# One transposing DMA in place of several, one more segment of x turned on TensorE, and an output bank lent to side work

## The chip, the cores and the metric

The kernel runs on one core of a Trainium2 chip. The metric is the device time of one execution in microseconds (us). TensorE (PE) multiplies, ScalarE (ACT) does the exponentials, VectorE (DVE) copies, normalises and reduces, GpSimd (POOL) masks, and SyncE (SP) issues every DMA. Each engine runs its own instructions strictly in order.

## What is computed

Two blocks on inputs of 2048 x 1024 bf16, their results side by side. A is plain attention with 32 heads of width 32. B is attention over four segments of 512 rows, causal within a segment, with a compressive memory carried from segment to segment and a gate per head.

```python
# A
qkv = (x @ wqkv) -> q, k, v per head
o_A = softmax(q @ k.T * Dh**-0.5) @ v;   out_A = o_A @ wo
# B, for s in range(4):
a_dot = softmax(q_s @ k_s.T * Dh**-0.5 + mask) @ v_s
a_mem = (phi(q_s) @ M) / (phi(q_s) @ z + 1e-6)
o     = g * a_mem + (1 - g) * a_dot        # g = sigmoid(beta)
M    += phi(k_s).T @ v_s;   z += sum(phi(k_s))   # phi(t) = t + 1 if t > 0 else exp(t)
out_B = concat(o) @ wo
```

## The kernel before

**Tiling.** Heads go in groups of four (128 columns of the weights), eight groups g. For A, each group has K, Q and V projections over four chunks c of 512 rows (`a_prep`), and then eight units of 256 queries each. For B there are 32 steps n = 8 s + g (`b_prep`), one for each segment s and group g, each with two units. A unit's scores come out of PE transposed, keys on partitions (`emit_scores`, L453); ACT takes the exponential of two or three PSUM banks at once into a ring PT of 20 slots (L470); then `emit_pv` (L519) multiplies by V and by ones, accumulating output and denominator in PSUM bank 5 (`OLB`). Banks 0 to 4 hold scores, and banks 6 and 7 (`PROJ`) serve everything else: projections, turns on PE, norms, the memory's products, output projections.

**Turns.** Projections need x with its columns on partitions. Of A's x, twelve of the sixteen 128-row tiles are loaded as they are into OTA, which is free at the start (`stage`), and turned on PE by `turn` (L373: eight transposes into one bank, then one copy out, on DVE and ACT alternately). B's first segment is turned likewise; its four tiles use places 12 to 15 of OTA. The last four tiles of A's x (chunk 3), and the later segments of B's x (`load_xB`, L318), come by eight transposing DMAs each of 512 x 128. V is projected transposed (columns on partitions), copied to VT (A) or SQB[1] (B), and turned by `turn_V` (L609) with four transposing DMAs of 128 x 128, each into its own tile of VA or VB; phi(K) is turned in the same way into PKt, for the memory's update (L811), in the first three segments.

**What sets the order.** The program is written out in Python before it runs. `schedule` keeps a model of when every engine will be free and when every operation ends. PE's modelled time is its clock: in each round it emits scores if a pair or triple of banks is free and the ring has room, else side work (generators such as `a_prep`, sorted by priority) or the next P V product, which are taken strictly in order from `pvq`. An operation is emitted only when the model has its operands ready. On the chip the recorded order is fixed, and semaphores hold an instruction (and all behind it on its engine) until its operands are really there. For a DMA, `Recorder.dma` books SP for `issue` us, then a shared pipe for `mb`/0.2 us, and 1.5 us more to landing; `turn_V` gives 0.6 us an issue and 0.06 MB, `load_xB` 1.3 us and 0.125 MB. Each of 24 DMA semaphores is used in turn, and a DMA waits for the last one on its own semaphore.

**Start.** `loads` issues on SP, in order: two of B's weights, B's four tiles, A's K weight, A's tiles 0 to 3, two more weights, A's tiles 4 to 11, eight transposing DMAs for chunk 3, the last weight, and four tiny DMAs that spread beta over partitions. Loads for the next step, the turns of V, phi(K) and the later segments of x, and the stores follow on the same queue, in the order in which the planner emits them. A first PV product needs its V tile, so the accumulation bank stands unused until V of B's first step is there.

Of the kernel before, what the change touches and what calls it, by code (L numbers as in the profile page):

```python
# [35 lines left out]
class Recorder:  # L36
# [58 lines left out]
    def dma(self, fn, r=(), w=(), issue=0.1, mb=0.25):  # L95
        c = self.ch_next
        self.ch_next = (c + 1) % self.NCH
        op = Op(f"D{c}", self.ch_n[c], fn)
        self.ch_n[c] += 1
        op.deps = self._deps(op.eng, r, w)  # L100
        if self.ch_last[c] is not None:
            op.deps.append(self.ch_last[c])
        self.ch_last[c] = op
        op.dma = c
        self._note(op, r, w)
        t = self.free["SP"]
        for d in op.deps:
            t = max(t, d.end + LAT)
        self.free["SP"] = t + issue
        self.pipe = max(self.pipe, t + issue) + mb / 0.2  # L110
        op.end = self.pipe + 1.5
        self.all.append(op)
        return op
# [121 lines left out]
class Kernel:  # L235
# [78 lines left out]
    def load_xB(self, s):  # L314
        b = s % len(self.xB)
        for i in range(NI):
            src = self.B_x[0][512 * s:512 * s + 512, P * i:P * i + P]
            self.R.dma(lambda e, i=i, src=src: e.dma_start(self.xB[b][:, i, :], src, transpose=True),  # L318
                       w=[("xB", b, i)], issue=1.3, mb=0.125)
        self.events.add(("xB", s))  # L320

    def stage(self, k):

        keys = [("OTA", k // 2, 4 * (k % 2) + c) for c in range(4)]
        return self.OTA[:, k // 2, 1024 * (k % 2):1024 * (k % 2) + 1024], keys

    def loads(self):
        R = self.R
        nc = self.nc
        for k in range(2):  # L330
            self.load_WB(k, 0)
        for k in range(4):
            dst, keys = self.stage(12 + k)
            R.dma(lambda e, k=k, dst=dst: e.dma_start(dst, self.B_x[0][P * k:P * k + P, :]), w=keys, issue=0.5)
        self.events.add(("xB", 0))
        self.load_WA(0, 0)
        for k in range(12):
            dst, keys = self.stage(k)
            R.dma(lambda e, k=k, dst=dst: e.dma_start(dst, self.A_x[0][P * k:P * k + P, :]), w=keys, issue=0.5)
            if k == 3:  # L340
                self.load_WA(1, 0)
                self.load_WB(2, 0)
        c = 3
        for i in range(NI):
            src = self.A_x[0][512 * c:512 * c + 512, P * i:P * i + P]
            R.dma(lambda e, i=i, c=c, src=src: e.dma_start(self.xA[:, i, 512 * c:512 * c + 512], src, transpose=True),
                  w=[("xA", i, c)], issue=1.3, mb=0.125)
        self.load_WA(2, 0)
        for h in range(4):
            src = bass.AP(tensor=self.B_beta.tensor, offset=self.B_beta.offset + h, ap=[[0, 32], [4, NG]])  # L350

            def f(e, h=h, src=src):
                with nc.allow_non_contiguous_dma(reason="tiny beta broadcast"):
                    return e.dma_start(self.beta[32 * h:32 * h + 32, 0:NG], src)
            R.dma(f, w=[("beta", h)], issue=0.5, mb=0.01)

# [26 lines left out]
    def constants(self):  # L383
# [19 lines left out]
        for i in range(2):  # L403
            pool(lambda e, i=i: e.memset(self.VB[i][:, :, :], 1.0), [("VB", i, t) for t in range(4)])
        pool(lambda e: e.memset(self.maskbd[:, :], 1.0), ["maskbd"])
# [94 lines left out]
    def emit_pv(self, u, st, part):  # L500
        R = self.R
        b = u.buf
        end = st == len(u.steps) - 1 and part == 1
        t, q0, w, off = u.steps[st][part]
        mms = []
        for ones in (False, True):
            for h in range(4):
                hs = slice(32 * h, 32 * h + 32)
                rhs = self.PT[:, u.p[(st, h)], off:off + w]
                if ones:  # L510
                    lhsT, o = self.ones[:, 0:32], self.ps[hs, OLB, QC + q0:QC + q0 + w]
                else:
                    lhsT = self.VA[b][:, t, hs] if u.kind == "A" else self.VB[b][:, t, hs]
                    o = self.ps[hs, OLB, q0:q0 + w]
                mms.append((o, lhsT, rhs, st == 0 and part == 0 and not ones))

        def f(e):
            for o, l, r, start in mms:
                ins = e.matmul(o, l, r, start=start, stop=end, skip_group_check=True)  # L519
            return ins  # L520
        vk = [("VA", b, t // 4, t % 4)] if u.kind == "A" else [("VB", b, t)]
        R.op("PE", f, r=[("PT", u.p[(st, h)]) for h in range(4)] + vk + ["ones"], w=[("ps", OLB)],
             cost=0.02 + 2 * w * 0.000417, mode="C")
        if part == 1:
            for h in range(4):
                self.ring_busy.discard(u.p[(st, h)])
        if end:
            x = u.seq % 2
            R.op("DVE", lambda e: e.tensor_copy(self.OL[x][:, :], self.ps[:, OLB, :]), r=[("ps", OLB)], w=[("OL", x)], cost=0.66)  # L529
            self.spawn(self.finish(u), -1, f"fin{u.kind}{u.kn}")  # L530
# [75 lines left out]
    def turn_V(self, src, skey, dst, dkey):  # L606

        for t in range(4):
            self.R.dma(lambda e, t=t: e.dma_start(dst[:, t, :], src[:, P * t:P * t + P], transpose=True),  # L609
                       r=[skey], w=[dkey + (t,)], issue=0.6, mb=0.06)  # L610

# [31 lines left out]
    def a_prep(self, g):  # L643
# [17 lines left out]
        def proj_V(c):  # L661
            vt, key = self.VT[c % 2], ("VT", c % 2)
            cs = slice(512 * c, 512 * c + 512)
            yield from self.proj_T(self.WA[2], ("WA", 2), lambda i: self.xA[:, i, cs], lambda i: ("xA", i, c), vt[:, :], key)
            self.turn_V(vt, key, self.VA[b][:, 4 * c:4 * c + 4, :], ("VA", b, c))
            self.events.add(("vA", g, c))
# [6 lines left out]
        for c in range(4):  # L673
            yield pace()
            if g == 0 and c < 3:
                yield from self.turn([(4 * c + t, self.xA[:, :, P * (4 * c + t):P * (4 * c + t) + P], [("xA", i, c) for i in range(NI)])
# [39 lines left out]
    def b_prep(self, n):  # L716
# [8 lines left out]
        if n == 0:  # L725
            yield from self.turn([(12 + t, self.xB[0][:, :, P * t:P * t + P], [("xB", 0, i) for i in range(NI)]) for t in range(4)])
        for k in range(2):
# [22 lines left out]
        yield from self.proj_T(self.WB[2], ("WB", 2), lambda i: self.xB[xb][:, i, :], xk, self.VTB[:, :], ("SQB", 1))  # L750
        self.turn_V(self.VTB, ("SQB", 1), VB[:, :, 0:P], ("VB", b))
        self.events.add(("vB", n))
# [48 lines left out]
        if s < 3:  # L801

            self.turn_V(PH[:, 0, :], ("PH", b), self.PKt, ("PKt",))
            yield ("t", R.lastw[("PKt", 3)].end)
            op = R.lastw[("PKt", 3)]
            bank = yield ("bank",)
            yield ("pe", op.end + 0.1)

            def fm(e, bank=bank):
                for tl in range(4):  # L810
                    ins = e.matmul(self.ps[:, bank, 0:129], self.PKt[:, tl, :], VB[:, tl, 0:129], start=(tl == 0), stop=(tl == 3))  # L811
                return ins
            R.op("PE", fm, r=[("PKt", t) for t in range(4)] + [("VB", b, t) for t in range(4)], w=[("ps", bank)], cost=0.4)
            op = R.op("DVE", lambda e, bank=bank: e.tensor_tensor(self.Mf[:, g, :], self.Mf[:, g, :], self.ps[:, bank, 0:129], ALU.add),
# [39 lines left out]
    def satisfied(self, req, now):  # L854
# [4 lines left out]
        if k == "bank":  # L859
            return any(b not in self.bank_busy and self.bank_end[b] <= now + 0.1 for b in PROJ)  # L860
        if k == "out":
# [11 lines left out]
    def resume(self, task, room=0.0):  # L873
        val = room
        if task.req[0] == "bank":
            now = self.R.free["PE"]
            val = next(b for b in PROJ if b not in self.bank_busy and self.bank_end[b] <= now + 0.1)
            self.bank_busy.add(val)
# [25 lines left out]
    def schedule(self):  # L904
# [7 lines left out]
        self.slot_end = {s: 0.0 for s in SLOTS}  # L912
        self.bank_busy, self.bank_end = set(), {b: 0.0 for b in PROJ}
        self.spawn(self.gates(), (-1, 0), "gates")
# [5 lines left out]
        while True:  # L920
# [37 lines left out]
            for what in (("pv", "side") if full else ("side", "pv")):  # L958
                if done:
                    break  # L960
                if what == "pv" and self.pvq:
# [3 lines left out]
                    v = ("vA", u.g, t // 4) if u.kind == "A" else ("vB", u.kn)  # L965
                    vk = ("VA", u.buf, t // 4, t % 4) if u.kind == "A" else ("VB", u.buf, t)
                    if v in ev and self.ready([vk]) <= now and all((st, h) in u.pend for h in range(4)) \
# [3 lines left out]
                            and (c <= room or len(self.ring_busy) > RING - 4):  # L971
                        self.emit_pv(u, st, part)
                        self.pvq.pop(0)
                        done = True
                elif what == "side":
# [8 lines left out]
            if cur is None and not self.qA and not self.qB and not self.pvq and not self.tasks:  # L984
                break
            bank = next((b for b in PROJ if b not in self.bank_busy and self.bank_end[b] <= now), None)
            if now < 45 and (RING - 1) not in self.ring_busy and not self.pos_ring and gap >= 0.3 and bank is not None:
# [57 lines left out]
```

## Time and profile before

| | us |
|---|---|
| median of three runs | 1438.58 |
| lowest and highest | 1428.88 and 1440.39 |
| the profiled execution | 1436.34 |
| its span in the profile | 1434.6 |
| granted TensorE clock, mean | 0.944 |
| bytes moved by DMA | 66.46 MB |

How to read it: the span is cut in windows, and for each engine the time in which it was busy stands in them. A row of the timeline gives the start, the length of a run of equal instructions, engine, line and operation, what it writes and reads, the count, and in brackets how long the engine stood idle before and what ended that. "SPq" rows are times in which SP's queue issued a DMA; they are not the time of the transfer. Where a run of instructions goes on without a bracket, the engine had no idle time worth naming before it.

### The profile page before, as it was taken

To read this page: it belongs to the slowest core of one execution; us is meant where nothing else is said; L and a number is where in the kernel's file an instruction comes from. 1 tells how busy PE (TensorE), PEld (TensorE's weight loads), DVE (VectorE), ACT (ScalarE), POOL (GpSimd) and SP (SyncE) were. 2 spreads that over 40 slices of the span, in tenths; PEclk is the share of its full clock that TensorE was granted. 3 is DMA by queue.
4 is the path that set the end of the run, shared out by engine and by line. 5 is a ranking of instruction groups with operands and counts; after the bars stand their busy time and mean duration, and the time that the engine had idled before them with its cause. 6 is when DMAs were issued, how large, how long until landed. Compare 5 with 4: busy or idle time off the path is not lost.

```text
span 1434.6 us, 37694 instructions
## 1 busy us (share of the span) xinstructions
PE 1258.9 (88%) x16930; PEld 511.7 (36%) x17155; DVE 833.0 (58%) x1389; ACT 1208.3 (84%) x1035; POOL 114.8 (8%) x209
## 2 busy tenths in 40 slices
PE   5678998898889997889769899899889989999998
PEld 3323333333333332333323333333334333333343
DVE  3446444645567646656446565466757758466675
ACT  3258798898889997899769999799989999999930
POOL 1000000101020101110001110001100101011110
PEclk9899899899999997989978999999999999999999
DMA  7224202112311012110320111211121011321111
GB/s 191 53 43 125 48 14 55 38 24 52 65 42 39 16 35 54 33 32 16 53 52 17 34 35 28 48 42 26 31 48 34 20 33 34 101 57 35 27 56 67
DMA packets 208770, 66.46 MB, mean 46 GB/s; under 512 B 200416, under 2 KB 200416, under 8 KB 208608
## 3 DMA queue, kind: packets, MB, share of 16 engines
q1 hardware_dynamic: 208608, 64.03, 19.1%
q8 instruction: 135, 2.21, 0.6%
q14 instruction: 27, 0.22, 0.1%
HBM read 39.85 MB, written 8.39 MB: 34 GB/s over the span
## 4 chain that ended last, share of the span: by engine, by line
ACT 54%; PE 26%; SPq 8%; DVE 5%; DMA 5%; issue 2%; DVEq 0%; ACTq 0%
ACT PT L470 53%; PE ps L593 13%; SPq L609 6%; PE ps L453 6%; PE ps L519 6%; SPq L318 2%; DMA PKt<-PH 1%; DVE OL L539 1%; DMA VB<-SQB 1%; DMA VA<-VT 1%; ACT E L763 1%; DMA WB<-in_B_wk_dram 1%; DVE OL L529 1%; DVE den L789 1%; PE ps L373 1%
## 5 line engine op out<-in xcount | busy, mean ns | idle before, releaser
L470 ACT ACTIVATE PT<-ps,cbA 128x1024 bf16<-128x1024 f32 (+1 forms) x832 | 1014.4, 1359 | 104.9 <-PE ps L453 93.9
L453 PE MATMUL ps<-QA,KA 32*128 32x256 bf16 x4096 | 334.6, 280 | 27.0 <-ACT PT L470 16.5
L519 PE MATMUL ps<-PT,ones 128*32 128x256 bf16 (+1 forms) x4864 | 323.2, 279 | 0.0
L519 PE MATMUL ps<-PT,VA 128*32 128x256 bf16 x4096 | 280.1, 285 | 8.9 <-DMA VA<-VT 6.3
L539 DVE RECIPROCAL OL<-OL 128x128 f32<-128x128 f32 x256 | 242.8, 949 | 5.4
L593 PE MATMUL ps<-xB,WB 128*128 128x512 bf16 x681 | 190.9, 397 | 29.5 <-issue 12.4
L593 PE MATMUL ps<-xA,WA 128*128 128x512 bf16 x685 | 189.0, 394 | 23.7 <-issue 11.8
L453 PEld LDWEIGHTS ps<-QA,KA 32*128 32x128 bf16 x4096 | 96.3, 93 | 303.7 <-ACT PT L470 230.7
L470 ACT ACTIVATE PT<-ps,cbB 128x768 bf16<-128x768 f32 (+3 forms) x160 | 170.6, 1183 | 35.9 <-PE ps L453 28.7
L490 POOL TENSOR_SCALAR_AFFINE_SELECT PT<-PT 128x512 bf16<-128x512 bf16 (+2 forms) x145 | 85.1, 601 | 1035.9 <-ACT PT L470 1034.6
L519 PEld LDWEIGHTS ps<-PT,VA 128*32 128x32 bf16 x4096 | 109.2, 96 | 147.2 <-issue 126.6
L519 PEld LDWEIGHTS ps<-PT,ones 128*32 128x32 bf16 x4864 | 132.6, 98 | 4.0 <-issue 0.2
L529 DVE COPY OL<-ps 128x512 f32<-128x512 f32 x128 | 86.1, 673 | 75.0 <-PE ps L519 74.3
L593 PEld LDWEIGHTS ps<-xB,WB 128*128 128x128 bf16 x768 | 63.7, 100 | 103.6 <-issue 47.0
L593 PEld LDWEIGHTS ps<-xA,WA 128*128 128x128 bf16 x768 | 61.8, 99 | 96.9 <-issue 37.2
L789 DVE RECIPROCAL den<-den 128x128 f32<-128x128 f32 x96 | 91.1, 949 | 2.2
L603 DVE CAST KQB<-ps 128x512 bf16<-128x512 f32 x64 | 43.3, 676 | 74.4 <-PE ps L593 73.8
L603 DVE CAST VT<-ps 128x512 bf16<-128x512 f32 x32 | 21.7, 677 | 91.3 <-PE ps L593 55.2
L838 DVE CAST outsb<-ps 128x512 bf16<-128x512 f32 x64 | 43.5, 682 | 51.0 <-PE ps L593 45.7
L593 PE MATMUL ps<-WoB,OTB 128*128 128x512 bf16 x238 | 63.4, 398 | 5.6 <-issue 2.7
L453 PE MATMUL ps<-KQB 32*128 32x256 bf16 (+1 forms) x768 | 59.6, 267 | 5.8 <-ACT PT L470 4.4
L593 PE MATMUL ps<-xA,OTA 128*128 128x512 bf16 x242 | 58.6, 380 | 3.5 <-issue 1.7
(72 smaller groups left out, 671.4 us busy)
## 6 DMA issues: line engine op xcount, KB each, us to landing
WB<-in_B_wk_dram SPq DMA_DIRECT2D x32, 256.0 KB, 3.1
WB<-in_B_wq_dram SPq DMA_DIRECT2D x32, 256.0 KB, 3.4
WB<-in_B_wv_dram SPq DMA_DIRECT2D x32, 256.0 KB, 3.1
out_dram<-outsb SPq DMA_DIRECT2D x32, 256.0 KB, 2.1
WA<-in_A_wqkv_dram SPq DMA_DIRECT2D x24, 256.0 KB, 3.8
OTA<-in_A_x_dram SPq DMA_DIRECT2D x12, 256.0 KB, 5.7
VB<-SQB SPq DMA_TRANSPOSE x128, 2.4
VA<-VT SPq DMA_TRANSPOSE x128, 2.4
```

Of the source, the lines that this page charges most:

```text
L318: self.R.dma(lambda e, i=i, src=src: e.dma_start(self.xB[b][:, i, :], src, transpose=True), w=[("xB", b, i)], issue=1.3, mb=0.125)
L453: ins = e.matmul(o, l, r, start=True, stop=True)
L470: op = R.op("ACT", lambda e: e.activation(self.PT[:, s0:s0 + n, 0:width], self.ps[:, banks[0]:banks[0] + n, 0:width], ACTF.Exp, bias=cb, s ...
L490: mo = R.op("POOL", lambda e, ap=ap, pat=pat: e.affine_select(ap, ap, pattern=pat, compare_op=ALU.is_ge, fill=0.0, base=0, channel_multipl ...
L519: ins = e.matmul(o, l, r, start=start, stop=end, skip_group_check=True)
L529: R.op("DVE", lambda e: e.tensor_copy(self.OL[x][:, :], self.ps[:, OLB, :]), r=[("ps", OLB)], w=[("OL", x)], cost=0.66)
L539: R.op("DVE", lambda e, Lq=Lq: e.reciprocal(Lq, Lq), r=[k], w=[k], cost=0.87)
L593: ins = e.matmul(o, l, rh, start=a, stop=z)
L603: op = self.R.op("DVE", lambda e: e.tensor_copy(dst, self.ps[:, bank, :]), r=[("ps", bank)], w=[dkey], cost=0.66)
L609: self.R.dma(lambda e, t=t: e.dma_start(dst[:, t, :], src[:, P * t:P * t + P], transpose=True), r=[skey], w=[dkey + (t,)], issue=0.6, mb=0.06)
L789: R.op("DVE", lambda e, cs=cs: e.reciprocal(self.den[:, cs], self.den[:, cs]), r=["den"], w=["den"], cost=0.9)
L838: op = R.op("DVE", lambda e, ns=ns, bank=bank, ob=ob: e.tensor_copy(self.outsb[ob][:, ns], self.ps[:, bank, :]), r=[("ps", bank)], w=[("ou ...
```

## The change

One transposing DMA does the work of four in `turn_V`, and one that of eight in `load_xB`; the planner's bookings and the names under which readiness is kept follow (a V or phi(K) tile is ready when the whole of it is). Chunk 3 of A's x is loaded as it is and turned on PE like the others; for that A's sixteen tiles fill OTA's places and B's four first tiles go to OTB[0]. The order of the first loads changes: beta comes after A's tile 3, and B's second weight after B's second tile. `self.banks` replaces PROJ: it holds banks 6 and 7 and, until the first P V product is emitted, bank 5 as well. The planner's pipe is booked at 0.25 MB a us.

```diff
-        self.pipe = max(self.pipe, t + issue) + mb / 0.2
+        self.pipe = max(self.pipe, t + issue) + mb / 0.25
...
     def load_xB(self, s):
         b = s % len(self.xB)
-        for i in range(NI):
-            src = self.B_x[0][512 * s:512 * s + 512, P * i:P * i + P]
-            self.R.dma(lambda e, i=i, src=src: e.dma_start(self.xB[b][:, i, :], src, transpose=True),
-                       w=[("xB", b, i)], issue=1.3, mb=0.125)
+        src = self.B_x[0][512 * s:512 * s + 512, :]
+        self.R.dma(lambda e: e.dma_start(self.xB[b][:, :, :], src, transpose=True),
+                   w=[("xB", b, i) for i in range(NI)], issue=5.0, mb=1.0)
...
     def stage(self, k):
-        keys = [("OTA", k // 2, 4 * (k % 2) + c) for c in range(4)]
-        return self.OTA[:, k // 2, 1024 * (k % 2):1024 * (k % 2) + 1024], keys
+        if k < 16:
+            return self.OTA[:, k // 2, 1024 * (k % 2):1024 * (k % 2) + 1024], [("OTA", k // 2, 4 * (k % 2) + c) for c in range(4)]
+        k -= 16
+        flat = self.OTB[0][:, :, :].rearrange("p j n -> p (j n)")
+        return flat[:, 1024 * k:1024 * k + 1024], [("OTB", 0, 2 * k), ("OTB", 0, 2 * k + 1)]
...
     def loads(self):
-        for k in range(2):
-            self.load_WB(k, 0)
+        self.load_WB(0, 0)
         for k in range(4):
-            dst, keys = self.stage(12 + k)
-            R.dma(lambda e, k=k, dst=dst: e.dma_start(dst, self.B_x[0][P * k:P * k + P, :]), w=keys, issue=0.5)
+            tile_in(16 + k, self.B_x[0][P * k:P * k + P, :])
+            if k == 1:
+                self.load_WB(1, 0)
         self.load_WA(0, 0)
-        for k in range(12):
+        for k in range(16):
+            tile_in(k, self.A_x[0][P * k:P * k + P, :])
             if k == 3:
+                for h in range(4):
+                    R.dma(f, w=[("beta", h)], issue=0.5, mb=0.01)
+            if k == 7:
                 self.load_WA(1, 0)
                 self.load_WB(2, 0)
-        c = 3
-        for i in range(NI):
-            src = self.A_x[0][512 * c:512 * c + 512, P * i:P * i + P]
-            R.dma(lambda e, i=i, c=c, src=src: e.dma_start(self.xA[:, i, 512 * c:512 * c + 512], src, transpose=True),
-                  w=[("xA", i, c)], issue=1.3, mb=0.125)
         self.load_WA(2, 0)
-        for h in range(4):
-            R.dma(f, w=[("beta", h)], issue=0.5, mb=0.01)
...
     def turn_V(self, src, skey, dst, dkey):
-        for t in range(4):
-            self.R.dma(lambda e, t=t: e.dma_start(dst[:, t, :], src[:, P * t:P * t + P], transpose=True),
-                       r=[skey], w=[dkey + (t,)], issue=0.6, mb=0.06)
+        self.R.dma(lambda e: e.dma_start(dst, src, transpose=True), r=[skey], w=[dkey], issue=1.4, mb=0.2)
...
-            if g == 0 and c < 3:
+            if g == 0:
                 yield from self.turn(...)
...
+        self.banks = PROJ + [OLB]
...
-                        self.emit_pv(u, st, part)
-                        self.pvq.pop(0)
-                        done = True
+                        if OLB in self.banks and OLB not in self.bank_busy:
+                            self.banks.remove(OLB)
+                        if OLB not in self.banks:
+                            self.emit_pv(u, st, part)
+                            self.pvq.pop(0)
+                            done = True
```

More of the change, by code (lines that the diff above doesn't have):

```diff
@@ L329, in loads, with tile_in, f @@
         nc = self.nc
-        for k in range(2):
-            self.load_WB(k, 0)
+        def tile_in(k, src):
+            dst, keys = self.stage(k)
+            R.dma(lambda e: e.dma_start(dst, src), w=keys, issue=0.5)
+        self.load_WB(0, 0)
         for k in range(4):
-            dst, keys = self.stage(12 + k)
-            R.dma(lambda e, k=k, dst=dst: e.dma_start(dst, self.B_x[0][P * k:P * k + P, :]), w=keys, issue=0.5)
+            tile_in(16 + k, self.B_x[0][P * k:P * k + P, :])
+            if k == 1:
+                self.load_WB(1, 0)
         self.events.add(("xB", 0))
         self.load_WA(0, 0)
-        for k in range(12):
-            dst, keys = self.stage(k)
-            R.dma(lambda e, k=k, dst=dst: e.dma_start(dst, self.A_x[0][P * k:P * k + P, :]), w=keys, issue=0.5)
+        for k in range(16):
+            tile_in(k, self.A_x[0][P * k:P * k + P, :])
             if k == 3:
+                for h in range(4):
+                    src = bass.AP(tensor=self.B_beta.tensor, offset=self.B_beta.offset + h, ap=[[0, 32], [4, NG]])
+                    def f(e, h=h, src=src):
+                        with nc.allow_non_contiguous_dma(reason="tiny beta broadcast"):
+                            return e.dma_start(self.beta[32 * h:32 * h + 32, 0:NG], src)
+                    R.dma(f, w=[("beta", h)], issue=0.5, mb=0.01)
+            if k == 7:
                 self.load_WA(1, 0)
                 self.load_WB(2, 0)
-        c = 3
-        for i in range(NI):
-            src = self.A_x[0][512 * c:512 * c + 512, P * i:P * i + P]
-            R.dma(lambda e, i=i, c=c, src=src: e.dma_start(self.xA[:, i, 512 * c:512 * c + 512], src, transpose=True),
-                  w=[("xA", i, c)], issue=1.3, mb=0.125)
-        self.load_WA(2, 0)
-        for h in range(4):
[L350 to L354, printed above, removed]
-            R.dma(f, w=[("beta", h)], issue=0.5, mb=0.01)
+        self.load_WA(2, 0)
     def late_loads(self):
@@ L403, in constants @@
         for i in range(2):
-            pool(lambda e, i=i: e.memset(self.VB[i][:, :, :], 1.0), [("VB", i, t) for t in range(4)])
+            pool(lambda e, i=i: e.memset(self.VB[i][:, :, :], 1.0), [("VB", i)])
         pool(lambda e: e.memset(self.maskbd[:, :], 1.0), ["maskbd"])
@@ L520, in f @@
             return ins
-        vk = [("VA", b, t // 4, t % 4)] if u.kind == "A" else [("VB", b, t)]
+        vk = [("VA", b, t // 4)] if u.kind == "A" else [("VB", b)]
         R.op("PE", f, r=[("PT", u.p[(st, h)]) for h in range(4)] + vk + ["ones"], w=[("ps", OLB)],
@@ L664, in proj_V @@
             yield from self.proj_T(self.WA[2], ("WA", 2), lambda i: self.xA[:, i, cs], lambda i: ("xA", i, c), vt[:, :], key)
-            self.turn_V(vt, key, self.VA[b][:, 4 * c:4 * c + 4, :], ("VA", b, c))
+            self.turn_V(vt[:, :], key, self.VA[b][:, 4 * c:4 * c + 4, :], ("VA", b, c))
             self.events.add(("vA", g, c))
@@ L725, in b_prep @@
         if n == 0:
-            yield from self.turn([(12 + t, self.xB[0][:, :, P * t:P * t + P], [("xB", 0, i) for i in range(NI)]) for t in range(4)])
+            yield from self.turn([(16 + t, self.xB[0][:, :, P * t:P * t + P], [("xB", 0, i) for i in range(NI)]) for t in range(4)])
         for k in range(2):
@@ L750, in b_prep @@
         yield from self.proj_T(self.WB[2], ("WB", 2), lambda i: self.xB[xb][:, i, :], xk, self.VTB[:, :], ("SQB", 1))
-        self.turn_V(self.VTB, ("SQB", 1), VB[:, :, 0:P], ("VB", b))
+        self.turn_V(self.VTB[:, :], ("SQB", 1), VB[:, :, 0:P], ("VB", b))
         self.events.add(("vB", n))
@@ L801, in b_prep @@
         if s < 3:
-            self.turn_V(PH[:, 0, :], ("PH", b), self.PKt, ("PKt",))
-            yield ("t", R.lastw[("PKt", 3)].end)
-            op = R.lastw[("PKt", 3)]
+            self.turn_V(PH[:, 0, :], ("PH", b), self.PKt[:, :, :], "PKt")
+            yield ("t", R.lastw["PKt"].end)
+            op = R.lastw["PKt"]
             bank = yield ("bank",)
@@ L812, in fm @@
                 return ins
-            R.op("PE", fm, r=[("PKt", t) for t in range(4)] + [("VB", b, t) for t in range(4)], w=[("ps", bank)], cost=0.4)
+            R.op("PE", fm, r=["PKt", ("VB", b)], w=[("ps", bank)], cost=0.4)
             op = R.op("DVE", lambda e, bank=bank: e.tensor_tensor(self.Mf[:, g, :], self.Mf[:, g, :], self.ps[:, bank, 0:129], ALU.add),
@@ L859, in satisfied @@
         if k == "bank":
-            return any(b not in self.bank_busy and self.bank_end[b] <= now + 0.1 for b in PROJ)
+            return any(b not in self.bank_busy and self.bank_end[b] <= now + 0.1 for b in self.banks)
         if k == "out":
@@ L876, in resume @@
             now = self.R.free["PE"]
-            val = next(b for b in PROJ if b not in self.bank_busy and self.bank_end[b] <= now + 0.1)
+            val = next(b for b in self.banks if b not in self.bank_busy and self.bank_end[b] <= now + 0.1)
             self.bank_busy.add(val)
@@ L912, in schedule @@
         self.slot_end = {s: 0.0 for s in SLOTS}
-        self.bank_busy, self.bank_end = set(), {b: 0.0 for b in PROJ}
+        self.banks = PROJ + [OLB]
+        self.bank_busy, self.bank_end = set(), {b: 0.0 for b in self.banks}
         self.spawn(self.gates(), (-1, 0), "gates")
@@ L965, in schedule @@
                     v = ("vA", u.g, t // 4) if u.kind == "A" else ("vB", u.kn)
-                    vk = ("VA", u.buf, t // 4, t % 4) if u.kind == "A" else ("VB", u.buf, t)
+                    vk = ("VA", u.buf, t // 4) if u.kind == "A" else ("VB", u.buf)
                     if v in ev and self.ready([vk]) <= now and all((st, h) in u.pend for h in range(4)) \
@@ L985, in schedule @@
                 break
-            bank = next((b for b in PROJ if b not in self.bank_busy and self.bank_end[b] <= now), None)
+            bank = next((b for b in self.banks if b not in self.bank_busy and self.bank_end[b] <= now), None)
             if now < 45 and (RING - 1) not in self.ring_busy and not self.pos_ring and gap >= 0.3 and bank is not None:
```

## The prediction

> **What bounds the kernel now.** I read the page's busy table first, then the windows of the whole span, then ACT's idle times in order, then SP's queue at the same places.
>
> ```profile
> span 1434.6 us, 37694 instructions
> PE 1258.9 (88%) x16930; PEld 511.7 (36%) x17155; DVE 833.0 (58%) x1389; ACT 1208.3 (84%) x1035; POOL 114.8 (8%) x209
> 0.00:80.00 80.00, 49.65 (x405) 25.01 (x413) 36.40 (x72) 21.46 (x24) 9.31 (x25) 0.91 0.50 118
> 80.00:150.00 70.00, 59.82 (x767) 22.46 (x779) 32.50 (x62) 58.48 (x50) 4.32 (x8) 0.93 0.33 82
> 150.00:1350.00 1200.00, 1073.35 (x15154) 431.55 (x15348) 710.25 (x1175) 1103.35 (x941) 95.06 (x166) 0.94 0.17 39
> 1350.00:1434.60 84.60, 76.05 (x607) 32.68 (x615) 53.84 (x82) 25.02 (x23) 6.09 (x11) 0.98 0.16 57
> 1100.00:1150.00 50.00, 46.16 (x710) 19.82 (x720) 36.50 (x61) 50.00 (x45) 7.41 (x13) 1.00 0.09 20
> ```
>
> Window rows give the length and then busy time of PE, PEld, DVE, ACT, POOL, the granted clock, the DMA share and GB/s. The exponentials on ACT set the pace: from 1100 to 1150 ACT is busy without a gap, PE for 46 of 50 us at full clock. ACT has 1208 us of work; the remaining 226 us are its idle time, and I divide them: 58.5 before 80 us, 11.5 from 80 to 150, 96.7 from 150 to 1350, 59.6 after. The last part is mostly output projections, which the change does not touch; I cost it at nothing.
>
> The middle 96.7 us decide. ACT's own timeline has 32 gaps of 1 us or more there, 84 us together; the first, the three of the worst stretch and the last but one are these, with PE and SP at the worst stretch below them:
>
> ```profile
> 158.97 2.54 ACT L470 ACTIVATE PT<-ps,cbA 128x1536 bf16<-128x1536 f32 x2 [4.58 <-PE ps L453]
> 710.89 2.62 ACT L470 ACTIVATE PT<-ps,cbA 128x1536 bf16<-128x1536 f32 x2 [7.60 <-PE ps L453]
> 733.73 1.11 ACT L470 ACTIVATE PT<-ps,cbA 128x1024 bf16<-128x1024 f32 x1 [5.64 <-PE ps L453]
> 749.21 1.11 ACT L470 ACTIVATE PT<-ps,cbA 128x1024 bf16<-128x1024 f32 x1 [6.00 <-PE ps L453]
> 1169.85 1.11 ACT L470 ACTIVATE PT<-ps,cbA 128x1024 bf16<-128x1024 f32 x1 [1.49 <-PE ps L453]
> 708.41 1.89 PE L593 MATMUL ps<-xA,WA 128*128 128x512 bf16 x4 [6.78 <-DVE VT L603]
> 732.01 0.59 PE L811 MATMUL ps<-VB,PKt 128*128 128x129 bf16 x4 [5.90 <-DMA PKt<-PH]
> 748.04 0.59 PE L811 MATMUL ps<-VB,PKt 128*128 128x129 bf16 x4 [6.17 <-issue]
> 689.21 12.09 SPq L318 DMA_TRANSPOSE xB<-in_B_x_dram  x8
> 701.35 15.25 SPq L609 DMA_TRANSPOSE VA<-VT  x12
> 725.29 5.37 SPq L609 DMA_TRANSPOSE PKt<-PH  x4
> 741.55 5.06 SPq L609 DMA_TRANSPOSE PKt<-PH  x4
> 153.96 5.59 SPq L609 DMA_TRANSPOSE VB<-SQB  x4
> ```
>
> Each ACT gap is a PE that stood still just before, with the next scores queued behind the waiting matmul. PE stood behind the fourth PKt quarter at 732 and 748 (the last of those issues ends at 730.66 and 746.61, landing follows 1.2 us later), and at 708 behind a VT buffer that VA's transposes were still reading, 12 us late because xB's eight issues stood ahead of them on SP. By SP's timeline, 30 of the 32 gaps lie within 12 us of a run of transposing issues. So the resource behind the middle gaps is SP's issue time.
>
> ```profile
> L609 SPq DMA_TRANSPOSE VB<-SQB x128: 1094/1232/7797, 32.4 to 1376.1; - x128
> L609 SPq DMA_TRANSPOSE VA<-VT x128: 1094/1232/2197, 83.1 to 1217.8; - x128
> L609 SPq DMA_TRANSPOSE PKt<-PH x96: 1093/1232/2420, 44.7 to 1095.9; - x96
> DMA to landing us min/median/max: 2.2/2.4/9.5
> L318 SPq DMA_TRANSPOSE xB<-in_B_x_dram x24: 1122/1262/2129, 121.4 to 699.2; - x24
> DMA to landing us min/median/max: 2.5/2.7/4.3
> ```
>
> (An issue row gives its time on SP in ns, min/median/max; the landing line under it gives the time from issue to landing, for all of L609 and then for L318.)
>
> **The change part by part.**
>
> *Turns of V and phi(K), four DMAs into one.* A turn of 128x512 now holds SP for 4 x 1.23 = 4.9 us, and its last quarter lands 3 x 1.23 + 2.4 = 6.1 us after the first issue. No row shows a transposing DMA from SBUF with four segments. Bounds: 1.26 us, the xB row, which moves the same 128 KB in one issue, four times a V quarter for 0.03 us more; and 4.9 us, were each segment to cost what it costs now. Less than 1.09 no transposing issue took. I take 1.26 and its landing of 2.7, because the bytes are equal: 88 turns x 3.66 = 322 us less on SP's queue and 3.4 us less from a finished VT to a usable V. What it loses: a matmul on the first V tile waits 2.7 instead of 2.4.
>
> [...]
>
> *The planner's bookings.* It booked 0.6 us an issue where SP took 1.23, hence a whole V at 4.2 us (2.4 + 0.3 + 1.5) where it came at 6.1. PE's order was written for that, and the scores behind the late matmul are the gaps. Now it books 1.4 + 0.8 + 1.5 = 3.7 where I expect 2.7, so PE should no longer be sent to wait there.
>
> *xB segments, eight into one* (three times). Bounds 1.26 and 8 x 1.26 = 10.1 us; the fastest transposing row moves 128 KB in 1.26 us, so for 1 MB I take 10.1 and gain nothing. What stands behind it on SP still waits about 10 us; this is late next.
>
> What of the 96.7 us goes? Where the gap is one turn's latency, (6.1 - 2.7) / 6.1 = 56% goes; where it is the queue of several turns, (4.92 - 1.26) / 4.92 = 74%; where a wait of 1 to 2 us vanishes under the planner's now generous booking, all of it. Bounds 54 and 92 us; I take 70%, **68 us**.
>
> *The start.* Rows of it:
>
> ```profile
> 15.42 12.04 SPq L346 DMA_TRANSPOSE xA<-in_A_x_dram  x8
> 28.13 2.06 SPq L354 DMA_DIRECT2D beta<-in_B_beta_dram  x4
> 32.38 11.62 SPq L609 DMA_TRANSPOSE VB<-SQB  x4
> 32.00:38.00 6.00, 1.62 (x16) 1.24 (x16) 0.69 (x1) 1.02 (x1) 0.00 (x0) 0.61 0.05 0
> 41.25 1.06 PE L593 MATMUL ps<-xB,WB 128*128 128x512 bf16 x2 [6.39 <-DMA WB<-in_B_wk_dram]
> 8.79 6.59 SPq L339 DMA_DIRECT2D OTA<-in_A_x_dram  x8
> 29.96 0.61 PE L373 MATMUL ps<-ident,OTA 128*128 128x128 bf16 x8
> 33.85 1.01 PE L373 MATMUL ps<-ident,OTA 128*128 128x128 bf16 x8 [1.21 <-ACT xA L378]
> 79.94 9.85 ACT L470 ACTIVATE PT<-ps,cbA 128x1536 bf16<-128x1536 f32 x8 [10.59 <-DVE cbA L669]
> 83.13 26.67 SPq L609 DMA_TRANSPOSE VA<-VT  x16
> ```
>
> ACT's A work begins at 79.94. PE is busy 49.7 of the 80 us before, so up to 30 us can be had. For 6 us after the beta loads no bytes move and 0.05 of 16 engines, that is one, is busy: the tiny transfers hold up all that follows, V's first turn (11.6 us on SP) and WB, for which PE waits 6.4 us. The move puts this behind A's fourth tile. Tiles 4 to 15, WA1 and WB2 then come up to 8 us later; PE reaches tile 4 at 29.96 now, and by the issue rows (0.82 us each) these tiles would be there at 22 to 30 with the hold-up in. I take 3 us lost again (bounds 0 and 8). The fourth segment: eight issues of 12.04 us leave SP, four loads of 0.82 come, and four turns of 0.61 to 1.01 on PE, 3 us; their copies (two on ACT, two on DVE) lie where ACT has no scores. The third bank takes most waits such as the 1.21 above: some 6 us over 20 turns (bounds 0 and 9); the first P V product then waits at most for one copy out, under 2 us. PE's clock, 0.61 in that window, recovers sooner: 3 us; first VB and PKt turns: 3 us. Sum 6.4 - 3 - 3 + 6 + 3 + 3 = 12.4, taken as **13 us** (bounds 5 and 22). From 80 to 150 ACT idles 11.5 us, mostly while sixteen VA issues take 26.7 us, which become four; I take **8 us** of it (bounds 3 and 11).
>
> **The sum.** 13 + 8 + 68 = 89. The profiled execution took 1436.34 us, 1.7 outside its span and 2.2 below the median of the three runs shown; 1436.3 - 89 = **1347 us**. With all lower bounds (62) it is 1374, with all upper (125) 1311.
>
> **The rivals.**
> 1. *The gaps stay as V's latency.* At 158.97 the gap began one turn's latency after VB's first issue at 153.96: the ring of exponentials was full, and P V products must wait for V however it comes. The planner now holds the first tile for 3.7 us where it held it 2.4. If that is the rule, only queue gaps such as 700 to 750 go: 34 of 96.7, 4 in the second part, 13 at the start: 51, so 1385. For it: the order of P V is strict, and PE has only 4 us in 50 to spare. Against: most of the gap time has several turns or a fourth quarter in it.
> 2. *Segments cost as before (slower).* One issue then holds SP 4.9 us and V lands at 6.1, while PE is sent at 3.7 and waits even on the first tile. Lateness against the booking was 6.1 - 4.2 = 1.9 and becomes 2.4, 0.5 us on each of 88 turns: 44 us more, less 13 at the start: 1436 + 31 = 1467. It decides once a merged issue holds SP over about 4.4 us (landing later than 3.7 + 1.9). For it: nothing shows a four-segment source in SBUF. Against: the xB row.
> 3. *The merged DMA is issued as four after all.* Then L609 still has 352 issues and only the start gains: 1436 - 13 = 1423; about as now.
>
> **How the numbers follow.** Forecast 0.72 (1311 to 1374), rival 1 0.18 (1374 to 1400), rival 3 0.04, rival 2 0.06. The range 1312 to 1400 holds the first two but for their ends. Over 1% (14 us, about what a measurement tells from no change) faster: 0.72 + 0.18 + 0.01; within 1%: 0.03; slower: 0.06.
>
> **What would show it.** L609 with 88 issues of about 1.3 us landing at 2.7 (issues near 4.9 mean rival 2, 352 issues rival 3); no PE wait of over 2 us at L811 for PKt; no DVE VT wait for VA; ACT above 45 of 50 from 700 to 750; A's first exponential near 67 us; no 6 us without bytes near 32. Wrong would be: gaps of 3 to 5 us beside every VB turn though the DMA is quick (rival 1), a PE wait on OTA near 20 us longer than 8, or an ACT tail over 62 us.

## The result, and the profile after

The changed kernel takes 1349.56 us (median of four runs, 1347.98 to 1352.14) against 1435.41 us of the kernel before in the same measurements: ratio 0.9406, 95% interval 0.9361 to 0.9452. The prediction was 1347, within 1312 to 1400. The profiled execution took 1352.14 us, 2.6 above the median, with a mean granted clock of 0.973 in place of 0.944.

First the page of the changed kernel (span, busy times), then the windows of its span. The third window ends with the last exponential of A's scores; before, the same point was 1364.1 us, and the last line is that window of the kernel before.

```profile
span 1350.1 us, 37376 instructions
PE 1232.8 (91%) x16968; PEld 509.2 (38%) x17194; DVE 831.7 (62%) x1391; ACT 1206.6 (89%) x1037; POOL 113.9 (8%) x207
```

```profile
0.00:80.00 80.00, 57.64 (x455) 29.28 (x461) 40.91 (x79) 26.74 (x28) 9.70 (x26) 0.91 0.47 122
80.00:150.00 70.00, 65.15 (x866) 26.27 (x875) 39.26 (x75) 59.92 (x52) 4.87 (x8) 0.99 0.38 91
150.00:1276.30 1126.30, 1049.23 (x15231) 426.26 (x15427) 704.24 (x1165) 1108.95 (x947) 93.28 (x162) 0.98 0.18 41
1276.30:1350.10 73.80, 60.75 (x427) 27.36 (x432) 47.25 (x73) 11.01 (x11) 6.10 (x11) 0.95 0.15 52
```

```profile
150.00:1364.10 1214.10, 1086.94 (x15347) 436.62 (x15542) 720.59 (x1190) 1117.45 (x953) 95.06 (x166) 0.95 0.17 39
```

Window length less ACT's busy time is ACT's idle time. By stage, with the same cut at the last exponential of A in both:

| ACT idle, us | 0 to 80 | 80 to 150 | 150 to last of A | tail | span |
|---|---|---|---|---|---|
| before | 58.5 | 11.5 | 96.6 | 59.6 | 1434.6 |
| after | 53.3 | 10.1 | 17.3 | 62.8 | 1350.1 |

Nearly the whole gain is in the middle. The start, from which the prediction wanted 21 us, gave 6.7; the middle gave 79 where 68 were forecast, and the tail took 3 back. The rows on SP of the changed kernel (issue time in ns, minimum, median and maximum, and for L609 the time from issue to landing):

```profile
L609 SPq DMA_TRANSPOSE VB<-SQB x32: 1190/1196/2558, 32.4 to 1290.5; - x32
L609 SPq DMA_TRANSPOSE VA<-VT x32: 1188/1191/2042, 90.0 to 1135.7; - x32
L609 SPq DMA_TRANSPOSE PKt<-PH x24: 1194/1267/2689, 34.6 to 994.8; - x24
DMA to landing us min/median/max: 2.4/2.5/5.3
L317 SPq DMA_TRANSPOSE xB<-in_B_x_dram x3: 4117/4390/4502, 102.7 to 622.1; - x3
```

There are 88 issues in place of 352, and one of 128x512 holds SP for 1.20 us by the median (1.27 for PKt), where one of 128x128 held it for 1.23. SP's share of the chain that ended last fell from 8% to 2% of the span. The worst stretch of before, 700 to 750 us with 29.9 us of ACT, is the first row here, and the changed kernel's the second:

```profile
700.00:750.00 50.00, 29.33 (x401) 11.19 (x403) 23.20 (x35) 29.89 (x25) 1.31 (x2) 0.80 0.23 48
700.00:750.00 50.00, 47.38 (x685) 19.24 (x692) 34.53 (x55) 50.00 (x45) 8.11 (x13) 1.00 0.15 35
```

In the changed kernel ACT has no gap in it, and PE's granted clock is 1.00 where it was 0.80. Over the whole middle the clock is 0.98 where it was 0.95, with PE standing still for 77 us of the window in place of 127; the runs don't part what of the gain comes through it. At the start things look different. A window, SP's rows, the row of the late weight on PE and A's first exponential:

```profile
12.00:18.00 6.00, 5.35 (x35) 2.68 (x34) 2.79 (x6) 1.02 (x1) 0.00 (x0) 1.00 0.06 2
```

```profile
7.93 1.91 SPq L351 DMA_DIRECT2D beta<-in_B_beta_dram  x4
9.88 7.80 SPq L335 DMA_DIRECT2D OTA<-in_A_x_dram  x4
26.43 0.82 PE L594 MATMUL ps<-xB,WB 128*128 128x512 bf16 x3 [4.29 <-DMA WB<-in_B_wv_dram]
84.31 8.59 ACT L471 ACTIVATE PT<-ps,cbA 128x1024 bf16<-128x1024 f32 x7
```

The six microseconds in which next to no bytes move, at a DMA share of 0.05 to 0.06, have moved with beta, from 32 us to 12 us (that share is as much as one engine of sixteen could do; the rows don't say which engines did it); four loads of x now stand on SP for 7.8 us behind them, and PE waits 4.3 us for a weight in place of 6.4. A's first exponential comes at 84.3 us, later than before (79.9), not at 67. PE was not idler for it: it is busy 57.6 of the first 80 us (before 49.7). Three of B's steps had their scores done by then, where it had been two.

### The profile page after: what moved, and what is told of

Read it like the earlier page. It is cut to its first block, busy times and chain, and to the rows that moved or that the text cites. A ratio compares the mean times of both kernels' runs of the same rounds, so it can differ in the third digit from the quotient of the medians.

```text
span 1350.1 us, 37376 instructions
## 1 busy us (share of the span) xinstructions
PE 1232.8 (91%) x16968; PEld 509.2 (38%) x17194; DVE 831.7 (62%) x1391; ACT 1206.6 (89%) x1037; POOL 113.9 (8%) x207
## 3 DMA queue, kind: packets, MB, share of 16 engines
q1 hardware_dynamic: 195712, 63.99, 20.2%
## 4 chain that ended last, share of the span: by engine, by line
ACT 66%; PE 23%; DVE 5%; SPq 2%; DMA 2%; issue 1%; POOL 0%; DVEq 0%
ACT PT L471 65%; PE ps L594 13%; PE ps L454 5%; PE ps L520 5%; DVE OL L540 2%; SPq L335 2%; ACT E L762 1%; DVE OL L530 1%; DMA PKt<-PH 1%; DVE outsb L837 1%; DMA WB<-in_B_wk_dram 0%; DMA out_dram<-outsb 0%; SPq L305 0%; DVE SQB L604 0%; DVE KQB L604 0%
## 5 line engine op out<-in xcount | busy, mean ns | idle before, releaser
L454 PE MATMUL ps<-QA,KA 32*128 32x256 bf16 x4096 | 328.7, 275 | 32.3 <-ACT PT L471 21.0
L520 PE MATMUL ps<-PT,ones 128*32 128x256 bf16 (+1 forms) x4864 | 315.0, 274 | 0.0
L520 PE MATMUL ps<-PT,VA 128*32 128x256 bf16 x4096 | 274.7, 282 | 1.5 <-DVE OL L530 0.8
L594 PE MATMUL ps<-xB,WB 128*128 128x512 bf16 x683 | 187.2, 393 | 23.6 <-issue 13.2
L594 PE MATMUL ps<-xA,WA 128*128 128x512 bf16 x679 | 181.0, 385 | 14.1 <-issue 12.7
```

The source lines that it names most:

```text
L454: ins = e.matmul(o, l, r, start=True, stop=True)
L594: ins = e.matmul(o, l, rh, start=a, stop=z)
```

## The experiments

Every kernel ran beside the kernel before, whose medians were 1431 to 1434 us.

**What of the gain is the turns?** The first asks for the turns alone, in the kernel before.

```diff
-        for t in range(4):
-            self.R.dma(... dst[:, t, :] <- src[:, P * t:P * t + P] ..., w=[dkey + (t,)], issue=0.6, mb=0.06)
+        self.R.dma(... dst <- src ..., w=[dkey + (t,) for t in range(4)], issue=1.4, mb=0.2)
```

> The kernel before with one part of the change: one transposing DMA per turn, booked 1.4 us and 0.2 MB. Theory T (the turns' time on SP's queue makes the gaps in the middle): ACT's idle time from 150 us to its last A work falls from 97 to 10 to 30 us and the kernel takes 1350 to 1375 us. Rival R (the other parts carry a large share of the gain): over 1390 us.

Measured: 1358.7 us, ratio 0.9469 (0.9439 to 0.9498). ACT idles 28.4 us in the middle, at the upper end of the theory. The turns are most of it; all else of the change brings 9 us more, with intervals that overlap at their edges.

**The queue's time, or the order that the planner wrote?** The wrong bookings of before and the long queue act together: PE waits because the order assumed an earlier V. The second kernel keeps the order exactly (each turn is booked as the four it replaces, and every quarter is held to be ready when it was) and issues one DMA. The third keeps the four DMAs and books each at 1.25 us.

```diff
 e2: one DMA on SP; planner's SP and pipe advanced as by four of 0.6 us,
     quarters ready at the times of the four
 e3: -  w=[dkey + (t,)], issue=0.6, mb=0.06)
     +  w=[dkey + (t,)], issue=1.25, mb=0.0)
```

> PE, DVE and ACT get exactly the instruction order of the kernel before; only the DMA of a turn is one in place of four. Theory Q (the queue's time on the chip is what costs): the waits of PE at the memory update and of DVE at VT vanish, 1355 to 1385 us. Rival B (the planner's too short bookings wrote a bad order, and a better order is what helped): over 1400 us, since the order is unchanged.

> The kernel before with four DMAs a turn, each booked at 1.25 us in place of 0.6, so that the order is written for what the queue really takes. Theory Q: the queue is as long as before, PE stands still less but the work comes as late: 1410 to 1440 us. Rival B: most of the gain appears, under 1390 us.

Measured: e2 1343.1 us, ratio 0.936 (0.9328 to 0.9391), below the range of theory Q; e3 1403.9 us, ratio 0.9787 (0.9759 to 0.9816), below Q's range and above B's. The windows from 150 us to A's last exponential, of e2 and then of e3:

```profile
150.00:1270.80 1120.80, 1080.77 (x15461) 427.51 (x15460) 711.58 (x1177) 1106.29 (x947) 93.69 (x164) 0.98 0.20 41
```

```profile
150.00:1321.20 1171.20, 1106.36 (x15539) 433.55 (x15539) 710.17 (x1179) 1115.68 (x954) 93.23 (x165) 0.96 0.18 40
```

ACT's idle time there is 14.5 us in e2 and 55.5 in e3, against 96.6. Not one instruction of PE, DVE or ACT stands elsewhere in e2, so the one DMA, by its shorter time on SP's queue (1.20 us in place of four times 1.23) and the earlier landing that goes with it (2.5 us after its issue), is by itself enough for the whole gain of the middle. Of the 29.0 us that PE waited for the turns at the memory update 0.8 are left, and of the 30.5 us that DVE waited to write VT until VA's transposes had read it 7.4, in one wait. But a truthful booking without any shorter queue would have had 30 us in all: 41 in the middle, of which the start and the tail took 11 back. The 82 us of e2 and the 41 of e3 overlap and can't be added. Both theories were too pure.

**The change without its turns.** All else of the change, with four DMAs a turn, booked right:

```diff
-        self.R.dma(... dst <- src ..., w=[dkey], issue=1.4, mb=0.2)
+        for t in range(4):
+            self.R.dma(... dst[:, t, :] <- src[:, P * t:P * t + P] ..., w=[dkey + (t,)], issue=1.25, mb=0.0)
```

> The changed kernel with turns by four DMAs, each booked at 1.25 us; all else of the change stays. Theory T: about 1410 to 1435 us, as the rest gave only some 5 us in the trace. Rival R: under 1380 us.

Measured: 1382.6 us, ratio 0.9645 (0.9611 to 0.9679), between the two. Compared with e3, which books alike, all else brings 21 us; on top of the turns (e1 to the changed kernel) it brings 9. Seen from the other side, the merged turns bring 75 us alone (e1) and 33 on top of all else. Of the 21 us, ACT's idle time shows 16 in the middle (55.5 to 39.4) and 9 in the tail, none at the start. That what is saved on SP is worth less where SP is no longer behind would explain it; no run takes it apart further.

**The start, part by part.** Three kernels take one part back each: the lent bank, beta's new place, the fourth chunk of x. The fourth takes away what beta does to the queue: one load of 64-byte rows in place of four loads of single 2-byte elements, in the same place and with the same order on PE.

```diff
 e5: -  self.banks = PROJ + [OLB]
     +  self.banks = list(PROJ)
 e6: the four beta loads at the end of loads()
 e7: -  ap=[[0, 32], [4, NG]]  ->  beta[32 * h:32 * h + 32, 0:NG], for h in range(4)
     +  ap=[[0, P], [1, 32]]   ->  beta[:, :], once; the gate's exponential picks column 4 g + h
 e8: -  for k in range(16): tile_in(k, ...)
     +  for k in range(12): tile_in(k, ...); chunk 3 by eight DMAs with transpose=True
```

> The changed kernel with banks 6 and 7 alone for side work. If the lent bank is worth the 6 us that the prediction gave it: A's first exponential 4 to 8 us later than in the changed kernel and 1354 to 1360 us. If it is worth nothing: A's first exponential within 2 us, and the time within 6 us of the changed kernel's on either side (the planner's order shifts with any edit).

> The changed kernel with the four beta loads last again. If the hold-up by beta costs PE about the same in either place: 6 us without bytes after the last loads, a PE wait of 4 to 7 us there, 1345 to 1356 us. If its new place ahead of A's tiles is what ate the start's gain: A's first exponential over 5 us earlier, under 1345 us.

> The changed kernel with beta as one load of 64-byte rows, one for each partition, in the same place; PE's order is unchanged, ACT has four small instructions for the gate in place of one. If the 2-byte pieces hold up the loads: no stretch without bytes before 40 us, no PE wait for WB near 26 us, A's first exponential 5 to 8 us earlier, 1341 to 1345 us. If the loads behind wait for something else: the same stretch stays, 1348 to 1351 us.

> The changed kernel with the fourth chunk of A's x by eight transposing DMAs in place of four loads and turns on TensorE. If the turns on TensorE help the start: A's first exponential 3 us or more later, 1353 to 1360 us. If x was there in time either way: four turns less on PE, A's first exponential 2 to 4 us earlier, 1344 to 1350 us.

| | us | ratio (interval) | A's first exponential | ACT idle to 150 us |
|---|---|---|---|---|
| changed kernel | 1349.6 | 0.9406 (0.9361 to 0.9452) | 84.3 | 63.3 |
| e5 bank not lent | 1358.0 | 0.9488 (0.9453 to 0.9524) | 92.5 | 71.1 |
| e6 beta last | 1348.0 | 0.9421 (0.9385 to 0.9457) | 79.8 | 59.0 |
| e7 beta in rows | 1344.4 | 0.9383 (0.9339 to 0.9427) | 79.7 | 58.5 |
| e8 chunk 3 by DMA | 1356.3 | 0.9474 (0.9433 to 0.9514) | 87.3 | 67.5 |

The lent bank is worth 8 us, all of it at the start. The turns of chunk 3 on TensorE gain 4 us of idle time there; the prediction had them cost 3. In e7 the dead stretch is gone, and so is PE's wait at 26 us, while A's first exponential is 4.6 us earlier where 5 to 8 were expected; the window of e7 is this:

```profile
12.00:18.00 6.00, 5.71 (x24) 2.38 (x22) 1.96 (x4) 0.26 (x1) 0.00 (x0) 0.69 1.08 303
```

303 GB/s in place of 2, with the same matmuls in the same order. e7 changes the number of the loads together with the size of their pieces; the loads of x beside them in this window come one after another without such a stretch, so that the small pieces are the likely cause, but no run parts the two. Beta's place changes the form of the hold-up (e6 has 4 us without bytes again, from 25 to 29 us, and a PE wait of 4.0 us behind them): e6 idles 4.3 us less at the start than the changed kernel, but by time the two can't be told apart. Of the four, only e5's interval lies apart from the changed kernel's; for the others the idle times say more than the medians, and in e5, e6 and e8 the planner's order shifts with the edit too.

**A truthful booking, and xB.** e1 and e2 differ only in booking (3.9 us for a whole turn, against 2.4 for the first quarter and 4.2 for the last) and in the order that follows; e2 is 16 us faster. Two kernels book the 2.7 us that a turn takes: e9, on top of e7, and e12, in place of e1's booking. e10 goes back to eight DMAs for a segment of xB.

```diff
 e9, e12: -  issue=1.4, mb=0.2)
          +  issue=1.2, mb=0.0)
 e10: +  for i in range(NI): self.R.dma(... self.xB[b][:, i, :] ..., issue=1.3, mb=0.125)
```

> The kernel with beta in rows (e7), and a turn booked at the 2.7 us that it takes (1.2 us of issue, no time in the pipe, 1.5 to landing) in place of 3.7. If the generous booking holds P V products and the memory's update back, as the gap of 16 us between the two kernels with the order of before would have it: 1330 to 1339 us. If the order alone shifts: 1340 to 1350 us.

> The kernel before with one transposing DMA per turn (e1), booked at the 2.7 us that it takes in place of 3.9 (1.4 + 0.2 MB at 0.2 MB a us + 1.5). If the generous booking made e1 16 us slower than the kernel with the order of before (e2): 1341 to 1348 us. If what order the planner falls into made it, booking or not: 1350 us or more.

> The changed kernel with a segment of xB by eight transposing DMAs in place of one: 10 us on SP's queue in place of 4.4, three times. If what stands behind them (turns of V) waits for that: idle time of ACT in the middle 5 to 15 us more, 1355 to 1365 us. If nothing urgent stands there: 1345 to 1354 us.

Measured: e12 1345.1 us (0.9391, 0.9357 to 0.9426), 13.6 less than e1 by the medians and 11 by the ratios, with intervals that lie apart: the generous booking was the cost there. In e9 it is 1341.5 us (0.9371, 0.9342 to 0.94), 2.9 less than e7, which the intervals don't tell apart; what the booking costs depends on the rest of the order. e10 takes 1355.2 us (0.9461, 0.9428 to 0.9494) with 20.2 us idle in the middle against 17.3: the one DMA for xB is worth some microseconds at most, and the intervals of e10 and the changed kernel overlap.

**The best of them.** The order of before, one DMA a turn (e2), and beta in rows at the end of the first loads; PE and DVE have the order of before, instruction for instruction.

> The kernel with PE's and DVE's order of before and one DMA a turn (e2), with beta in rows at the end of the first loads. If the hold-up by beta is worth its PE wait there (6.4 us at 41 us): that wait is gone and 1335 to 1339 us. If the start is set by other waits: 1341 to 1345 us.

Measured: 1334.3 us, ratio 0.9317 (0.9285 to 0.9349), just under the first range and below the changed kernel's interval; that of e2 it overlaps (9 us apart by the medians, 6 by the ratios). Of e11, the window in which the kernel before moved no bytes, and its first exponential of A:

```profile
32.00:38.00 6.00, 4.83 (x56) 3.08 (x56) 1.39 (x2) 1.73 (x2) 0.00 (x0) 0.72 0.32 69
```

```profile
70.78 15.73 ACT L473 ACTIVATE PT<-ps,cbA 128x1536 bf16<-128x1536 f32 x13 [11.22 <-DVE cbA L681]
```

In e2 PE waited 5.9 us at 39.7 for the second step's weight; that wait is gone, and A's first exponential is 8 us earlier than in e2 (79.2). The granted clock of the first 80 us is 0.98 in e11's profile and 0.89 in e2's, so that part of the 8 us may be the clock's; whether it rose because PE stood still less isn't shown. Of the three rearrangements at the start, none is in this kernel.

## Why the prediction was right, and where not

**The bound and the mechanism** held. ACT sets the pace, its gaps in the middle came from the turns' transposing issues on SP, and e2 shows it with the order on PE, DVE and ACT unchanged: the DMA alone takes the idle time there from 96.6 to 14.5 us. Of the signs that the prediction named, the issues and the stretch from 700 to 750 came out. A's first exponential near 67 us did not, and one sign of being wrong came true: ACT's tail, 62.8 us, is over 62.

**The merged turn** was taken at 1.26 us and a landing of 2.7, from the xB row with equal bytes; it took 1.20 (PKt 1.27) and 2.5. So rival 2 falls: four segments from SBUF in one issue held SP about as long as one segment did, 1.20 us (1.27) against 1.23. Rival 3 falls with 88 issues.

**What of the middle goes** was mis-sized: 70% was taken, 82% went (79 of 96.6). The two rates that the prediction worked out, 56 and 74%, give at most 72 us; beyond them only its third case is left, waits that vanish whole, and its upper bound of 92 has no working. Rival 1, that the gaps are V's own latency and stay, is refuted by the same number. What share the planner's order has was left open: e3 shows that 41 of the 96.6 us go by a truthful order alone, with the queue as long as ever. The prediction named the booking but gave it no term of its own.

**"Generous booking"** was counted as a gain. e1 and e12 show the other side: 1.2 us too much on each turn cost 11 to 14 us there. That P V products which could run are held back is the likely reason, but the runs show only that the order differs: e1 idles more than e12 at the start (4 us), in the middle (7) and in the tail (8).

**xB** was bounded at 1.26 and 10.1 us and taken at 10.1, as if no transposing DMA could move more than 128 KB in 1.26 us. It took 4.4. The step from the fastest row to the fastest possible failed: eight times the bytes held SP 3.5 times as long here, 4.39 us against 1.26.

**The start** failed as a sum, 21 us forecast and 6.7 measured. By its terms: the third bank (6) is worth 8 by e5. The turns of chunk 3 (a loss of 3) are a gain of 4 by e8. The move of beta (a gain of 3.4) shows as a loss of 4.3 us of idle time by e6, and with the hold-up gone altogether (e7) the start has 4.8 less. Of the clock's term (3) nothing shows: the first 80 us have 0.91 in both kernels. The first VB and PKt turns (3) and the part from 80 to 150 (8, measured 1.4) belong to the turns, and e1, with the turns alone, takes 6.8 us off the start (70.1 to 63.2). With the bank, chunk 3 and beta's move the parts would make over 14, but the changed kernel idles 63.3 us, no less than e1: they don't add up. The trace shows where the order went another way. A's first exponential, taken as the mark, moved back while PE was busier, and B's third step came in ahead of A; the runs don't show what in the planner put it there, nor that this alone ate the rest. The prediction summed waits on PE as if the work behind them stayed in place.

**The tail** was costed at nothing, since the change doesn't touch the output projections, and lost 3 us. It goes with the order: in e2, with the order of before, it is 59.0 us, in the changed kernel 62.8.

The errors at the start (14 us too much), in the middle (11 too little) and in the tail (3 us lost, taken as nothing) nearly cancel. That the total came within 3 us is luck; the bound, the cause and the rough size of the middle were not.

## What to carry to other kernels

Where an engine issues DMAs one after the other, count its time per instruction and look at what stands behind: here some 330 us of issue time (352 issues of 1.23 us at the median less 88 of 1.20), on a queue that was not the busiest resource, made 82 us of idle time on the bounding engine. An order that is written ahead should book what the trace shows for an operation, neither less (e3: 30 us) nor more (e12: 11 to 14 us, while e9 can't be told from e7). And edits to such a planner are judged best with the order held fixed, since parts taken one by one don't add up.

## What the runs showed that was not expected

SP's time for a transposing DMA is nearly the same at three sizes and longer at the fourth, by the medians: 1.23 us for 128x128, 1.20 for 128x512 out of SBUF, 1.26 for 512x128 out of HBM, 4.39 for 512x1024 out of HBM (4.12 to 4.50 over the changed kernel's three). And four loads of single 2-byte elements, 2 KB in all, stopped nearly everything behind them for 4 to 7 us in every kernel that had them (4 us in e6, 7 in e12), each time with a DMA share of about 0.05. Where they stood last among the first loads, V's first transposing issue behind them held SP for 7.3 us (e6) to 8.1 us (e3), 7.8 in e2; in e11, which differs from e2 by the loading of beta alone, it is 1.9. With the same 32 values as one load of 64-byte rows there is no such stretch: 303 GB/s from 12 to 18 us in e7, and 69 from 32 to 38 in e11.
